# Values of a pair placed behind the next pair's scores, and the last values eight steps later

## The chip, the cores and the metric

The kernel runs on one core of a Trainium2 chip. The metric is the device time of one execution in microseconds (us). A core has a matrix engine (TensorE, PE in the profile, with its weight loads shown as PEld), a vector engine (VectorE, DVE), an activation engine (ScalarE, ACT), a general engine (GpSimd, POOL) and a sequencer that issues transfers (SyncE, SP). [...]

## The reference, cut to what matters

An attention over 4 batches, 8 heads, 768 tokens of 64 elements, followed by a Fourier mix and a two-layer network. Of the attention, per batch and head:

```python
block, window = (32, 16)
k_sum = k.reshape(B, H, nb, block, D).max(axis=3)
v_sum = v.reshape(B, H, nb, block, D).mean(axis=3)
scores_l = scale * q @ k.T        # kept where |i - j| < 16 ("near")
scores_s = scale * q @ k_sum.T + log(block)   # one column per block of 32 ("sums")
a = softmax(concat(scores_l, scores_s))
out = a @ concat(v, v_sum)
...
mixed = real(fft2(x)); u = x + mixed; un = layernorm(u)
result = u + relu(un @ w_ch1) @ w_ch2
```

All of it is in float32.

## The kernel before, in words

**What is threaded into what.** The heads of a batch are worked on in four pairs, g = 0 to 3. The attention of batch b + 1 is threaded into the dense layers of batch b. `gen_attention(b)` is a generator that is advanced step by step: every `yield` ends a step. For batches 2 and 3 the loop at the end, `drive((most, 44, 0), (gen_attention(b + 1), 80, 0))`, advances the dense work 44 steps while the attention takes 80. The dense steps are 16 of `gen_hidden(b, 0)` (tiles hx, hy, hz; line 1368), 12 of `gen_out(b, 0)` (tiles ox, oy, oz; line 1437; four steps for each of i = 0, 1, 2, with seven products in them) and 16 of `gen_hidden(b, 1)`. For batch 1 there is one attention step to five dense ones and ten of the conversion of the weights (`gen_weights`). After that stage `gen_out(b, 1)` and the Fourier mix of batch b + 1 (`gen_fourier`) run together.

**A pair.** `prepare` turns k and q (for batch 3 and all but the first pair of batch 2 with VectorE's transpose, line 711) and takes the block maxima. `scores(b, g)` makes the near scores: 48 matmuls on quarters of TensorE's array (64 rows by 64 columns, line 791) into two PSUM banks, an exp on ScalarE for each half (line 797) and a product with the mask `near` on VectorE. `sum_scores` makes the scores against the block maxima: four matmuls of 64 by 32 (tile ss, line 808) and an exp. `scale_sums` brings the block sums of v into place (tile vs: one matmul, line 814, and two scalings on ScalarE, line 816). `values(b, g, ...)` multiplies: 48 matmuls of 64 by 32 (tile av, line 826) with v from `vw_bufs`, six more with vs (line 831), then on VectorE two reciprocals and two products into x. `load_values` then issues four transfers on SP that refill `vw_bufs[g % 2]` for the pair after the next; they have to wait for that buffer's last reader.

**Buffers.** The attention's PSUM tiles (scores, ss, vs, av) share four banks (`abank`). The probabilities `p` have two buffers, `vw` two, `vs` one, and the natural q and k tiles four together.

**The order.** Apart from the first batch's attention, no order is written out by hand. A planner in the framework fixes each engine's order before the kernel runs: of the instructions that it believes ready, the one created first goes first. `tc.issue_after` adds an edge on one engine.

**The end of a batch's attention (b > 1).** After `values(b, 3)`, `turn_tiles` (lines 954 and 955) stores two tiles of x to DRAM on POOL's queue and gathers them back mirrored (tile xr). Some steps later `fold_batch` adds halves of x on VectorE, its second step reading xr; the Fourier mix needs the fold.

**Step numbers before, for batches 2 and 3**: scores at steps 5, 17, 27 and 37, values at 12, 22, 32 and 42, the fold from 59, its reader of xr at 60.

Of the kernel before, what the change touches and what calls it, by code (L numbers as in the profile page):

```python
# [488 lines left out]
def _main_program(ctx, tc, q, k, v, moe_w_ch1, moe_w_ch2, out):  # L489
# [9 lines left out]
    NP = H // 2  # L499
# [56 lines left out]
    def abank(shape, name):  # L556
        return psum.tile(shape, FP, tag="attn", bufs=4, name=name)
# [12 lines left out]
    def tt(out, in0, in1, op):  # L570
        return nc.vector.tensor_tensor(out=out, in0=in0, in1=in1, op=op).ins  # L571
# [92 lines left out]
    def load_values(b, g):  # L664
        if is_wide(b):
            load_wide_values(b, g)
            return
        load_narrow_values(b, g)

    def load_wide_values(b, g):  # L670

        vw, off = wide_vw(g), v[b, 2 * g].offset
        for r0, r1, i0, i1 in ((0, WK, 1, NQ - 1), (W, WK, 0, 1), (0, WK - W, NQ - 1, NQ)):
            for e in range(2):
                fetch(out=vw[r0:r1, e, i0:i1, 0:D],
                      in_=bass.AP(v.tensor, off + (S * e + QB * i0 - W + r0) * D,
                                  [[D, r1 - r0], [QB * D, i1 - i0], [1, D]]))

    def load_narrow_values(b, g):


        vw = vw_bufs[g % 2]
        if g < 2 and is_wide(b - 1):
            nc.gpsimd.memset(vw[:, :, D:D1], 1.0)
        for e in range(2):
            off = v[b, 2 * g + e].offset
            for h in range(2):
                r, i = 64 * (e ^ h), NB2 * h
                last = (b, g, e, h) == (B - 1, NP - 1, 1, 1)
                if last:  # L690

                    fetch(out=vw[r + 64 - W:r + 64, i:nb - 1, 0:D],
                                      in_=bass.AP(v.tensor, off + (BLOCK * i + 64 - 2 * W) * D,
                                                  [[D, W], [BLOCK * D, NB2 - 1], [1, D]]))
                n = 64 - W if last else 64
                fetch(out=vw[r:r + n, i:i + NB2, 0:D],
                                  in_=bass.AP(v.tensor, off + (BLOCK * i - W) * D, [[D, n], [BLOCK * D, NB2], [1, D]]))
# [104 lines left out]
    def sum_scores(b, g, p):  # L802
        km, qt = km_bufs[g % 2], nat[b, g]
        ps = abank([P, S2], f"ss_{b}_{g}")
        for h in range(2):
            for e in range(2):
                rows, r = slice(D * e, D * (e + 1)), 64 * (e ^ h) + 32 * h
                nc.tensor.matmul(ps[r:r + 32, :], km[rows, :], qt[rows, S2 * h:S2 * (h + 1)], start=True, stop=True)  # L808
        nc.scalar.activation(out=p, in_=ps, func=AF.Exp, scale=SC)

    def scale_sums(b, g):
        ps = abank([P, D], f"vs_{b}_{g}")
        vb, pick = sums[b, g]
        nc.tensor.matmul(ps, pick, vb, start=True, stop=True)
        for r in range(2):
            nc.scalar.activation(out=vs[:, r, 0:D], in_=ps, func=AF.Identity, scale=half_of[:, r:r + 1])

    def values(b, g, p, pm, x):
        vw = vw_bufs[g % 2]
        av = [abank([P, NST, D1], f"av_{b}_{g}_{r}") for r in range(2)]  # L820
        for t in range(NST):
            h = t // HT
            for j in range(4):
                for r in range(2):
                    rows, i = slice(64 * r, 64 * (r + 1)), 4 * t + j
                    nc.tensor.matmul(av[r][32 * j:32 * (j + 1), t, :], p[rows, h, i - NB2 * h, :], vw[rows, i, :],  # L826
                                     start=(t == 0), stop=False, skip_group_check=True)
        for t in range(HT):
            for r in range(2):
                rows = slice(64 * r, 64 * (r + 1))  # L830
                ins = nc.tensor.matmul(av[r][:, t:t + HT + 1:HT, :], pm[rows, P * t:P * (t + 1)], vs[rows],  # L831
                                       start=False, stop=(t == HT - 1), skip_group_check=True)
        marks["av", b, g] = ins.ins
        for r in range(2):
            rc = rec[:, b * NP + g, r]
            nc.vector.reciprocal(out=rc, in_=av[r][:, :, D])
            xo = x[:, 0, P * g + D * r:P * g + D * (r + 1)]
            xo = bass.AP(xo.tensor, xo.offset, [list(xo.ap[0]), [HT * DM + D * (1 - 2 * r), 2], [DM, HT], [1, D]])
            tt(xo, av[r].rearrange("p (h t) d -> p h t d", h=2)[:, :, :, 0:D],
               rc.rearrange("p (h t) -> p h t", h=2)[:, :, :, None].to_broadcast([P, 2, HT, D]), ALU.mult)  # L840
# [3 lines left out]
    def following(b, g, n):  # L844
        i = b * NP + g + n
        return divmod(i, NP) if i < B * NP else None
# [101 lines left out]
    def turn_tiles(b, x):  # L948


        xr = apool.tile([P, 2, NQ, QB], FP, tag="p", name=f"xr_{b}").rearrange("p e n c -> p (e n c)")
        back[b] = xr = xr[:, 0:2 * DM].rearrange("p (i d) -> p i d", i=2)
        turned = dpool.tile([P, 2, DM], FP, name=f"turned_{b}")
        nc.gpsimd.dma_start(out=turned, in_=x[:, 2:NST:HT, :])
        nc.gpsimd.indirect_dma_start(out=xr.rearrange("p i d -> p (i d)"), out_offset=None,
                                     in_=turned.rearrange("p i d -> p (i d)"),
                                     in_offset=bass.IndirectOffsetOnAxis(ap=mirror[:, 0:1], axis=0))
# [29 lines left out]
    def gen_attention(b):  # L987
        x = bpool.tile([P, NST, DM], FP, tag="x", bufs=2, name=f"x_{b}")
        x_of[b] = x
        held = None  # L990
        if b == 2:
            load(2, 1)
            load(2, 2)
        if b > 1:
            yield
            yield
            with tc.issue_after(marks["load"]):
                block_sums(b, 0)
            for _ in range(2):
                yield  # L1000
        for g in range(NP + 1):
            n1, n3 = (following(b, g, n) for n in (1, 3))
            if held:
                if b > 1:
                    scale_sums(b, g - 1)
                values(b, g - 1, *held, x)
                if n1 and b > 1:
                    load_values(*n1)
            if g == NP and b > 1:
                turn_tiles(b, x)  # L1010
                for _ in range(17):
                    yield
                rooms[b] = room(f"fold_{b}")
                steps = fold_batch(b, split_fold(b, rooms[b]))
                while True:
                    with tc.issue_after(marks["dense"]):
                        done = next(steps, steps) is steps
                    if done:
                        break
                    yield  # L1020
            elif held:
                for _ in range(5 if b > 1 else 1):
                    yield
            if g < NP:
                with tc.issue_after(marks["tile"]) if (b, g) == (1, 0) else ExitStack():
                    held = scores(b, g)
                if (b, g) == (1, 1):
                    with tc.issue_after(marks["mx", 0]):
                        key_maxima(g)
                sum_scores(b, g, held[1])  # L1030
            if g and n1 and b == 1:
                load_values(*n1)
            if g == 1 and b > 1:
                block_sums(b, 1)
            if g == NP and b > 1:
                return
            yield
            if g == NP:
                return
            for _ in range(2 if g == 0 and b > 1 else 0):  # L1040
                yield
            if (b, g) == (1, 0):
                for h in range(2):
                    with tc.issue_after(marks["un", 0]):
                        tt(held[0][:, h], held[0][:, h], near[:, h], ALU.mult)
            if n1:
                prepare(*n1, *((1,) if b > 1 else ()))
            if b == 1:
                scale_sums(b, g)
            if b > 1:  # L1050
                yield
                yield
                if n1:
                    prepare(*n1, 0)
            if n3 and not (b == 1 and n3 > (2, 0)):
                load(*n3)
            yield
            if b > 1:
                yield
# [561 lines left out]
```

## Time and profile before

| what | value |
|---|---|
| median of 3 runs | 794.84 us (793.83 to 795.17) |
| profiled execution, its own time | 793.7 us |
| span of the profiled execution | 791.9 us |
| busy: PE, DVE, ACT, POOL | 776.3, 492.0, 224.7, 47.9 us |
| PE busy in 274 to 375 us (attention of batch 2) | 100.72 of 101 us |
| PE busy in 460 to 525 us (attention of batch 3) | 64.48 of 65 us |
| near score matmuls, line 791 | 1152 records |
| value matmuls, lines 826 and 831 | 1152 and 144 records |

A float32 matmul leaves two records in the trace. Starts of matmuls are measured while their ends are modelled, so that in the timeline a group's duration runs over the next group's start; differences of starts are used below. In the page's chain of waits a share is the part of the span that belongs to an engine or a line on the chain of work that ended last. In a list of groups, "out<-in" names the tile that is written and those that are read.

### The profile page before, as it was taken

How to read it: one execution, taken by the hardware profiler on the slowest of the kernel's cores; microseconds unless marked ns; L12 is line 12 of the kernel's file. 1: busy time of each engine (PE TensorE's matmuls, PEld its weight loads, DVE VectorE, ACT ScalarE, POOL GpSimd, SP SyncE). 2: the span in 40 equal slices, each digit the busy share in tenths (PEclk: the TensorE clock that was granted, in tenths of full speed). 3: DMA queues.
4: the chain of work that ended last, by engine and by line, in shares of the span. 5: the costliest groups of instructions: out<-in, count | busy, mean ns of one | idle time of the engine just before them, and what ended most of it. 6: DMA issues, size and time to landing. Idle time of an engine off the chain costs nothing.

```text
span 791.9 us, 14352 instructions
## 1 busy us (share of the span) xinstructions
PE 776.3 (98%) x5920; PEld 562.9 (71%) x5920; DVE 492.0 (62%) x1019; ACT 224.7 (28%) x491; POOL 47.9 (6%) x85
## 2 busy tenths in 40 slices
PE   8998999999999999999999999999999999999997
PEld 6777655445588866787578866788569875886686
DVE  5899988787988556752758544653677623533352
ACT  3564757226525022100236012200226111001200
POOL 0000000000000020200210020300120000000000
PEclk9999999999999999999999999999999999999999
DMA  9999787695956179976342169610614153106001
GB/s 212 189 262 246 190 268 190 210 284 201 240 186 152 46 206 263 218 110 184 137 153 94 54 208 211 183 55 11 243 37 140 54 215 134 51 0 233 0 28 56
DMA packets 133353, 121.82 MB, mean 154 GB/s; under 512 B 94464, under 2 KB 114912, under 8 KB 133088
## 3 DMA queue, kind: packets, MB, share of 16 engines
q1 hardware_dynamic: 132160, 118.53, 54.0%
q0 software_dynamic: 576, 2.10, 0.8%
q8 instruction: 48, 0.79, 0.4%
q10 hardware_dynamic: 544, 0.20, 0.1%
q14 instruction: 25, 0.20, 0.1%
HBM read 97.22 MB, written 23.59 MB: 153 GB/s over the span
## 4 chain that ended last, share of the span: by engine, by line
PE 88%; DVE 5%; ACT 4%; DMA 2%; issue 1%; DVEq 0%
PE hx L1368 19%; PE ox L1437 18%; PE hz L1368 9%; PE oz L1437 9%; PE hy L1368 5%; PE o L1414 5%; PE oy L1437 5%; PE y L1252 3%; PE sc L791 2%; PE mx L1211 2%; PE av L826 2%; PE unt L1342 1%; PE av L831 1%; DMA qn<-in_q_dram 1%; PE ss L808 1%; ACT kt L727 1%
## 5 line engine op out<-in xcount | busy, mean ns | idle before, releaser
L1368 PE MATMUL hx<-u,w 128*128 128x384 f32 x512 | 185.4, 491 | 2.4 <-ACT h L1385 1.0
L1368 PEld LDWEIGHTS hx<-u,w 128*128 128x128 f32 x512 | 95.2, 190 | 71.3 <-ACT p L797 3.8
L1368 PE MATMUL hz<-u,w 128*128 128x384 f32 x256 | 93.0, 486 | 0.0
L1437 PE MATMUL oz<-w,s 128*128 128x256 f32 x336 | 81.3, 380 | 0.0
L1437 PE MATMUL ox<-w,s 128*128 128x256 f32 x336 | 80.1, 380 | 0.0
L1437 PE MATMUL ox<-w,h 128*128 128x256 f32 x336 | 79.6, 381 | 0.0
L571 DVE TENSOR_TENSOR x<-ox,x 128x256 f32<-128x256 f32 x84 | 35.5, 422 | 66.2 <-PE ox L1437 65.9
L1368 PEld LDWEIGHTS hz<-u,w 128*128 128x128 f32 x256 | 48.6, 190 | 33.9
L1437 PEld LDWEIGHTS ox<-w,h 128*128 128x128 f32 x336 | 63.1, 190 | 10.8 <-issue 1.2
L1437 PEld LDWEIGHTS ox<-w,s 128*128 128x128 f32 x336 | 63.2, 190 | 9.1 <-DVE x L571 0.3
L1437 PEld LDWEIGHTS oz<-w,s 128*128 128x128 f32 x336 | 63.3, 190 | 8.9 <-DVE x L571 0.4
L1379 ACT COPY h<-hx 128x384 f32<-128x384 f32 x32 | 15.3, 477 | 191.6 <-PE hx L1368 191.5
L571 DVE TENSOR_TENSOR h<-hy,h 128x384 f32<-128x384 f32 x32 | 17.8, 557 | 48.9 <-PE hy L1368 48.8
L1368 PE MATMUL hy<-u,w 128*128 128x384 f32 x128 | 46.8, 487 | 0.0
L571 DVE TENSOR_TENSOR h<-hx,h 128x384 f32<-128x384 f32 x32 | 17.8, 556 | 45.2 <-PE hx L1368 44.0
L1414 PE MATMUL o<-w,h 128*128 128x512 f32 x96 | 42.2, 595 | 0.7 <-DVE w L571 0.7
L1398 ACT ACTIVATE h<-hx 128x384 f32<-128x384 f32 x32 | 15.7, 489 | 89.4 <-PE hx L1368 89.4
L1437 PE MATMUL oy<-w,h 128*128 128x256 f32 x168 | 40.1, 380 | 0.0
L571 DVE TENSOR_TENSOR x<-oz,x 128x256 f32<-128x256 f32 x42 | 17.8, 423 | 30.4 <-PE oz L1437 30.1
L1368 PEld LDWEIGHTS hy<-u,w 128*128 128x128 f32 x128 | 24.2, 190 | 17.1 <-DVE h L571 0.7
L1437 PEld LDWEIGHTS oy<-w,h 128*128 128x128 f32 x168 | 31.8, 190 | 4.4
L1414 PEld LDWEIGHTS o<-w,h 128*128 128x128 f32 x96 | 18.0, 190 | 23.6 <-issue 20.7
(166 smaller groups left out, 1072.5 us busy)
## 6 DMA issues: line engine op xcount, KB each, us to landing
w<-dw SPq DMA_DIRECT2D x44, 896.0 KB, 5.6
words<-in_moe_w_ch_dram SPq DMA_DIRECT2D x32, 512.0 KB, 5.8
dw<-w SPq DMA_DIRECT2D x12, 896.0 KB, 7.0
vw<-in_v_dram SPq DMA_DIRECT2D x47, 192.0 KB, 6.2
out_dram<-x SPq DMA_DIRECT2D x23, 256.0 KB, 2.0
vb<-in_v_dram SPq DMA_DIRECT2D x24, 192.0 KB, 7.2
kn<-in_k_dram SPq DMA_DIRECT2D x9, 384.0 KB, 6.3
qn<-in_q_dram SPq DMA_DIRECT2D x9, 384.0 KB, 6.9
```

What stands on the lines that cost most here:

```text
L571: return nc.vector.tensor_tensor(out=out, in0=in0, in1=in1, op=op).ins
L727: nc.scalar.copy(out=dst[D * e:D * (e + 1), s:S:2], in_=ps[D * s:D * (s + 1)])
L791: nc.tensor.matmul(ps[h][r:r + 64, i, :], kt[rows, o:o + 64], qt[rows, o:o + BLOCK], start=True, stop=True)
L808: nc.tensor.matmul(ps[r:r + 32, :], km[rows, :], qt[rows, S2 * h:S2 * (h + 1)], start=True, stop=True)
L826: nc.tensor.matmul(av[r][32 * j:32 * (j + 1), t, :], p[rows, h, i - NB2 * h, :], vw[rows, i, :], start=(t == 0), stop=False, skip_group_ch ...
L1211: nc.tensor.matmul(out, y[:, g], table, start=False, stop=True, skip_group_check=True)
L1252: nc.tensor.matmul(y, fgs[b][par][:, st, P * g:P * (g + 1)], fs[par][:, g % 2, st, :], start=(st == 0), stop=(st == n - 1))
L1368: ins = nc.tensor.matmul(ps, w[:, a, kk, :], u[:, r, kk, :], start=start and kk == 0, stop=stop and kk == 1, skip_group_check=True)
L1379: nc.scalar.copy(out=c11, in_=X)
L1398: nc.scalar.activation(out=c21, in_=X, func=AF.Relu)
L1414: nc.tensor.matmul(ps, h[:, n, hf, P * t:P * (t + 1)], wt[2, b, j][:, 2 * hf:2 * hf + 2, :], start=(n, hf) == (0, 0), stop=(n, hf) == (NC ...
L1437: nc.tensor.matmul(ps, left[a][:, n, :], wt[2, b, j][:, r, :], start=start and n == 0, stop=stop and n == NC - 1, skip_group_check=True)
```

## The change

For the joined pairs (1 to 3 of batches 2 and 3, and pair 3 of batch 1) the values of the pair before are no longer issued ahead of the scores but behind `sum_scores`. For batches 2 and 3 `scale_sums` of that pair is then issued ahead of the scores, and `load_values` behind the values. The five steps between the old place and the scores stay, so that values 0, 1 and 2 go from steps 12, 22 and 32 to 17, 27 and 37. The last values of batches 2 and 3 wait eight steps more (42 to 50), `turn_tiles` with them, and the pause from there to the fold is nine steps instead of 17, so that the fold keeps its place.

```diff
         for g in range(NP + 1):
             n1, n3 = (following(b, g, n) for n in (1, 3))
-            if held:
+            joined = (1 if b > 1 else 3) <= g < NP
+            if b > 1 and g == NP:
+                for _ in range(8):
+                    yield
+            if held and not joined:
                 if b > 1:
                     scale_sums(b, g - 1)
                 values(b, g - 1, *held, x)
...
             if g == NP and b > 1:
                 turn_tiles(b, x)
-                for _ in range(17):
+                for _ in range(9):
                     yield
...
             if g < NP:
+                past = held
+                if joined and b > 1:
+                    scale_sums(b, g - 1)
                 with tc.issue_after(marks["tile"]) if (b, g) == (1, 0) else ExitStack():
                     held = scores(b, g)
                 if (b, g) == (1, 1):
                     with tc.issue_after(marks["mx", 0]):
                         key_maxima(g)
                 sum_scores(b, g, held[1])
+                if joined:
+                    values(b, g - 1, *past, x)
+                    if n1 and b > 1:
+                        load_values(*n1)
```

## The prediction

> **What bounds the kernel now.** I read the page first: the busy shares, then the chain that ended last.
>
> ```profile
> PE 776.3 (98%) x5920; PEld 562.9 (71%) x5920; DVE 492.0 (62%) x1019; ACT 224.7 (28%) x491; POOL 47.9 (6%) x85
> PE 88%; DVE 5%; ACT 4%; DMA 2%; issue 1%; DVEq 0%
> ```
>
> TensorE sets the time: 88% of the chain is its work. So the change is worth what it takes off TensorE's own row, or adds there. Next I read the timeline of TensorE where batch 2's attention is threaded through batch 1's dense work (274 to 375 us); columns are start, duration, engine, line, operation, count (two records a matmul).
>
> ```profile
> 281.32 1.45 PE L1368 MATMUL hz<-u,w 128*128 128x384 f32 x4
> 282.71 1.60 PE L791 MATMUL sc<-qt,kt 64*64 64x32 f32 x96
> 284.24 0.85 PE L808 MATMUL ss<-qt,km 64*32 64x384 f32 x8
> 285.02 1.56 PE L1368 MATMUL hx<-u,w 128*128 128x384 f32 x4
> 286.41 1.45 PE L1368 MATMUL hz<-u,w 128*128 128x384 f32 x4
> ...
> 292.86 1.45 PE L1368 MATMUL hz<-u,w 128*128 128x384 f32 x4
> 294.15 0.33 PE L814 MATMUL vs<-vbs,sel 96*128 96x64 f32 x2
> 294.42 1.20 PE L826 MATMUL av<-vw,p 64*32 64x65 f32 x96
> 295.55 0.94 PE L831 MATMUL av<-vs,p 64*128 64x130 f32 x12
> 296.42 1.56 PE L1368 MATMUL hx<-u,w 128*128 128x384 f32 x4
> ```
>
> Durations overlap, so I take differences of starts. A dense group of four records takes 1.29 us (292.86 to 294.15). Before a score visit it takes 1.39 (281.32 to 282.71): 0.10 to go in. After it, 1.39 again (285.02 to 286.41): 0.10 to come out. A score visit thus occupies 0.10 + 1.53 + 0.78 + 0.10 = 2.51 us. A value visit goes in at no visible cost and leaves at the same 0.10: 0.27 + 1.13 + 0.87 + 0.10 = 2.37.
>
> The same timeline at batch 2's last values shows a visit that has come apart:
>
> ```profile
> 353.88 0.33 PE L814 MATMUL vs<-vbs,sel 96*128 96x64 f32 x2
> 354.14 0.54 PE L826 MATMUL av<-vw,p 64*32 64x65 f32 x24
> 354.62 2.86 PE L1437 MATMUL ox<-w,h 128*128 128x256 f32 x12
> 357.41 0.88 PE L826 MATMUL av<-vw,p 64*32 64x65 f32 x48
> 358.22 0.93 PE L831 MATMUL av<-vs,p 64*128 64x130 f32 x6
> 359.08 1.13 PE L1437 MATMUL ox<-w,h 128*128 128x256 f32 x4
> 360.14 0.54 PE L826 MATMUL av<-vw,p 64*32 64x65 f32 x24
> 360.62 0.93 PE L831 MATMUL av<-vs,p 64*128 64x130 f32 x6
> ```
>
> From 353.88 to the next dense product at 361.48 are 7.60 us, in which lie 16 dense records of 0.216 (eight take 1.726 elsewhere), 3.45 us. The values cost 7.60 - 3.45 + 0.10 = 4.25 us where a whole visit costs 2.37. The planner cuts where it believes an operand isn't there; the cuts at 12 and 36 of 48 matmuls fit the four transfers of vw that these matmuls read.
>
> [...] That fits the broken visit: its first 12 matmuls take 0.48 us, 40 ns each, against 1.13/48 = 24 ns where both row halves alternate. [...] the two mask products take 2.76 us at 321.71, under four GpSimd additions (321.24 to 325.63), and 1.03 elsewhere.
>
> **The change part by part.** *Joining.* At pairs 1 to 3 of batches 2 and 3 the vs matmul (1), 48 + 6 value matmuls, and with them ACT's two scalings, DVE's two reciprocals and two products and SP's four vw loads go five steps later; only vs stands ahead of the scores. One way out (0.10) and one way in (0.10, vs taking dense-to-vs at nothing and vs-to-next at the 0.27 it has now) go: 6 x 0.20 = **-1.2 us**. Batch 1's values of pair 2 move from 144.87 to behind 166.55: **-0.15**, by the same rates.
>
> *Banks.* Four banks serve six tiles in a visit: vs, two scores, ss, two av. The first av takes the bank of vs, free after ACT's scalings (0.52 us) long before. The second takes the first scores' bank, free after an exp: that begins 0.11 after the scores (321.08 to 321.19) and takes 0.49, so it ends at 0.60, and ss covers 0.78. Margin 0.18. If it took the second exp (ends at 0.98 by 321.19 + 0.87 = 322.06), 0.20 a visit would show. Bounds 0 to 6 x 0.2 = 1.2; below nothing is excluded, as no such wait exists now. I take **+0.3**.
>
> *DVE and ACT behind the visit.* Reciprocals and products are 0.27 + 1.02 = 1.29 us. They begin when av ends, and the first dense group needs 1.39 us before DVE is wanted: hidden; were DVE late by the mask products, the next group's 1.29 still covers. One stall goes: at 324.99 TensorE waited for DVE, 1.73 instead of 1.29 after 323.26, **-0.44**; the av visit now stands there while DVE finishes. The like stall at 471.41 (batch 3, pair 0, not joined) stays.
>
> *SP.* vw(2,2) was issued from 304.37; it must now wait for av behind the scores that start at 303.06, to some 306.5: 2 us, with weight stores, weight loads and k and q loads behind it. Those k and q are for the next batch (460 us on), the weights for 326 on: cost 0, bound 1. vw(3,3), which held SP 8.6 us before the weight loads at 500.72, falls behind the weight load of dense step 13 (attention step 24, between old place 22 and new 27): a gain in slack only. In batch 1 the vw(2,0) loads (161.25 to 167.93) must wait for av to some 168.5; raw weights for DVE's conversion (168.03) stand behind. Bounds 0 to 2 us, the products "o" having waited for DVE w 2.5 us in all in that stage; I take **+0.3**.
>
> *Last values eight steps later.* Steps are 44 dense to 80: step 42 falls after 23 dense steps, step 50 after 27, both just ahead of an i's last product. The place is thus seven products later, ahead of the ox that starts at 370.38 now. vw(2,3) gets eight steps more, and asks at most five later, so I expect the visit whole: 4.25 - 2.37 = **-1.88**. What it risks is the turning on POOL:
>
> ```profile
> 362.69 0.87 POOL L954 DMA_DIRECT2D turned<-x  x1 [35.61 <-DVE x L571]
> 369.89 1.06 POOL L955 DMA_INDIRECT xr<-turned,mirror  x1 [6.33 <-DMA turned<-x]
> ```
>
> From the first to the gather's landing are 7.20 + 4.6 = 11.8 us; in batch 3 4.0 + 4.6 = 8.6. After the change the visit starts at 370.38 - 4.25 - 1.04 (0.6 of three joins, 0.44) = 365.1, ends 2.27 later, DVE 1.3 later, POOL starts near 369.0, xr lands near 380.8. DVE's reader of xr stands at 384.30 now and near 384.30 - 2.92 = 381.4 then: margin 0.6. If late, DVE's next products wait: 0.24 us is idle ahead of the one at 387.70, and TensorE covers 1.29 - 0.56 = 0.73 more. Bounds 0 to 1 (a landing 2 us later); I take 0, since nine steps remain. Nothing else on POOL is queued behind until the fold.
>
> **Sum**: -1.2 - 0.15 + 0.3 - 0.44 + 0.3 - 1.88 = -3.1 us. The profiled execution took 793.7 (span 791.9); it would take 790.6. The median shown is 794.84, 1.1 above it: **791.8 us**.
>
> **Rivals.** *The gains are eaten*: the last values stay apart (their loads move with them), or the margins of 0.18 and 0.6 fail. The joins alone are -1.2: 793.6, within 793.3 to 796.4. For it: the loads do move five steps. Against it: the last values move eight.
> *Visits come apart* (the slower side): with six tiles on four banks the planner finds av not ready after ss and puts dense products between, as at 354.62. The joined visit then does not exist. Each costs 1.88 more instead of 0.20 less. Two broken turn -3.1 into +1.1, not to be told from no change; three give 794.84 - 3.1 + 3 x 2.08 = 798.0, all six some 804. From three on the kernel is slower. For it: sc and ss had to part in batch 1 (82.52, 101.71), where banks were scarce. Against it: in batches 2 and 3 vs and av stay whole though av's last six wait for ACT, and only vw broke one.
>
> **Numbers.** Likeliest 0.58, its own range 790.0 (no bank or SP cost, and a little of the 471.41 stall) to 793.2. Eaten 0.21: 793.3 to 796.4. Apart 0.21: 796.4 to 804, half of it below 798. About 0.2% (1.6 us) is what a measurement of this kernel tells from no change. The range 790.0 to 798.0 leaves out the tail of the third case and a little below the first.
>
> **What would show it.** Right: in TensorE's timeline vs, sc, ss, av, av without a dense group between, six times; one way out each; the last av of batch 2 as x96; no gap at 324.99. Wrong: dense groups inside a visit, PE waiting for ACT p L797 ahead of av, or DVE fold waiting for xr.

## The result, and the profile after

The changed kernel takes **808.03 us** (median, 803.75 to 811.71) where the kernel before, run beside it, takes 795.0 (793.33 to 796.02): a ratio of 1.0158, 95% interval 1.0136 to 1.018. The prediction was 791.8, within 790.0 to 798.0. It was wrong: the kernel became slower by 13 us. The profiled execution took 807.59 us, with a span of 805.8 (before: 793.7 and 791.9). The six runs of the changed kernel spread over 1%, the six of the kernel before over 0.3%; 25 later ones of the kernel before spread over 0.9% (792.79 to 800.12).

The page after has these lines in the places of the two that the prediction began with (busy time of the engines; chain of work by engine), and between them, from the list of DMA queues, a line that was passed over before (packets, MB, share):

```profile
PE 778.3 (97%) x5920; PEld 566.7 (70%) x5920; DVE 491.9 (61%) x1019; ACT 225.0 (28%) x491; POOL 47.0 (6%) x85
...
q8 instruction: 48, 0.79, 0.4%
...
PE 86%; DVE 5%; ACT 4%; DMA 3%; issue 2%; SPq 0%; DVEq 0%
```

TensorE's work is the same, 778.3 us against 776.3, yet the span is 13.9 longer. So what was added is idle time, or time at a lower clock. "issue", waiting for nothing that the profile shows, has doubled to 2%. The list of TensorE's waits (waiting operation, what ended the wait, us in total, times, longest) says where:

```profile
PE hx L1379 <- DVE h L571: 4.5, 2, 3.9
PE av L826 <- issue: 3.9, 3, 2.5
PE av L831 <- issue: 3.5, 1, 3.5
```

Before, these were 0.8, 0.6 and none. First, though, the joins. A visit is a stay of TensorE at the attention's products between two groups of dense ones; in a joined visit it takes scores and values in one go. Here is TensorE's timeline in batch 2, the joined visit of pair 1, then that of pair 2, then the last values.

```profile
308.68 0.33 PE L814 MATMUL vs<-vbs,sel 96*128 96x64 f32 x2
308.94 1.60 PE L791 MATMUL sc<-qt,kt 64*64 64x32 f32 x96
310.48 0.85 PE L808 MATMUL ss<-qt,km 64*32 64x384 f32 x8
311.12 1.20 PE L826 MATMUL av<-vw,p 64*32 64x65 f32 x96
312.25 0.94 PE L831 MATMUL av<-vs,p 64*128 64x130 f32 x12
313.12 1.56 PE L1379 MATMUL hx<-u,w 128*128 128x384 f32 x4
...
326.63 0.85 PE L808 MATMUL ss<-qt,km 64*32 64x384 f32 x8
327.28 0.71 PE L826 MATMUL av<-vw,p 64*32 64x65 f32 x47
330.47 0.73 PE L826 MATMUL av<-vw,p 64*32 64x65 f32 x49 [2.48 <-issue]
...
375.44 1.20 PE L826 MATMUL av<-vw,p 64*32 64x65 f32 x96
```

The first visit is what the change was meant to bring: vs, sc, ss, av, av with no dense product between, 4.44 us to the next dense product and 0.11 for the way out, 4.55 in all, where two visits cost 2.51 + 2.37 = 4.88. The second stops for 2.5 us in the middle of 96 like records. The last line is batch 2's last value visit, now whole. Of the six joined visits of batches 2 and 3 five have this order. In the sixth, pair 3 of batch 3, the planner cut the scores in three, with dense products between:

```profile
520.36 0.31 PE L791 MATMUL sc<-qt,kt 64*64 64x32 f32 x6
...
523.39 0.41 PE L791 MATMUL sc<-qt,kt 64*64 64x32 f32 x10
...
530.84 1.37 PE L791 MATMUL sc<-qt,kt 64*64 64x32 f32 x80
```

By differences of starts these scores take 1.87 us instead of 1.53, with two more ways in and two more ways out (0.42): some 0.4 us more than a whole join saves. In batch 1 such a stop stands in the joined visit, and something follows it:

```profile
168.31 0.71 PE L831 MATMUL av<-vs,p 64*128 64x130 f32 x6
172.50 1.02 PE L831 MATMUL av<-vs,p 64*128 64x130 f32 x6 [3.48 <-issue]
173.45 13.44 PE L1425 MATMUL o<-w,h 128*128 128x512 f32 x28
186.73 1.45 PE L1379 MATMUL hx<-u,w 128*128 128x384 f32 x4
```

The 28 records of o are followed by the next group 13.28 us after their start. In the kernel before it was 12.12:

```profile
166.55 12.28 PE L1414 MATMUL o<-w,h 128*128 128x512 f32 x28
178.67 1.45 PE L1368 MATMUL hx<-u,w 128*128 128x384 f32 x4
```

A table by stretches (us of the stretch, busy time of TensorE, granted clock, DMA share, GB/s) shows why:

```profile
169.00:172.40 3.40, 0.02 (x1) 1.00 1.18 257
172.40:175.80 3.40, 3.30 (x9) 0.50 1.15 182
```

After a stretch of idleness TensorE ran one stretch at half its clock. The trace's clock records put the half-clock stretches of this execution, up to its last products, at 80.25, 172.41 and 582.01, each 3.41 us long, so each costs up to 1.71. The third follows the wait at batch 3's turned copy (timelines of GpSimd, VectorE and TensorE):

```profile
561.26 0.75 POOL L954 DMA_DIRECT2D turned<-x  x1 [51.23 <-DVE ok L1585]
571.48 1.03 POOL L955 DMA_INDIRECT xr<-turned,mirror  x1 [9.46 <-ACT h L1409]
...
578.56 0.69 DVE L571 TENSOR_TENSOR fold<-xr 128x512 f32<-128x512 f32 x1 [4.67 <-DMA xr<-turned,mirror]
...
582.24 4.41 PE L1379 MATMUL hx<-u,w 128*128 128x384 f32 x8 [3.86 <-DVE h L571]
```

From issuing the copy to having xr are 17.3 us (write 9.4 us to its landing, gather 7.1). In the kernel before it took 8.4 (the gather landed 4.4 us after its issue):

```profile
523.65 0.75 POOL L954 DMA_DIRECT2D turned<-x  x1 [21.98 <-DVE x L571]
527.65 1.03 POOL L955 DMA_INDIRECT xr<-turned,mirror  x1 [3.26 <-DMA turned<-x]
```

The **ledger** of the two profiled executions, 13.9 us apart in span:

| what | us |
|---|---|
| three gaps inside joined visits (3.48 + 2.48 + 0.79) | +6.75 |
| the wait for xr | +3.86 |
| two half-clock stretches, behind the gap of 3.48 and behind the wait for xr | +3.42 |
| before any moved product: waits for q until 40 us (1.2), the half-clock stretch at 80.25 (1.6) | +2.8 |
| five whole joins, 0.33 each | -1.65 |
| the sixth, cut | +0.4 |
| batch 2's last values | -1.88 |
| the stall at 324.99, gone | -0.44 |
| sum | 13.3 |

0.6 is not accounted for. The 2.8 belongs to the execution rather than to the change: up to 144.87 of before TensorE's products stand in the same order in both kernels, and a version without any join (below) has a half-clock stretch at 78.22 too.

### The profile page after: what moved, and what is told of

The parts are those of the page before. It is cut to its first block, busy times and chain, and to the rows that moved or that the text cites. A ratio compares the mean times of both kernels' runs of the same rounds, so it can differ in the third digit from the quotient of the medians.

```text
span 805.8 us, 14349 instructions
## 1 busy us (share of the span) xinstructions
PE 778.3 (97%) x5920; PEld 566.7 (70%) x5920; DVE 491.9 (61%) x1019; ACT 225.0 (28%) x491; POOL 47.0 (6%) x85
## 4 chain that ended last, share of the span: by engine, by line
PE 86%; DVE 5%; ACT 4%; DMA 3%; issue 2%; SPq 0%; DVEq 0%
PE hx L1379 19%; PE ox L1448 18%; PE hz L1379 9%; PE oz L1448 9%; PE hy L1379 5%; PE o L1425 5%; PE oy L1448 4%; PE y L1263 3%; PE sc L791 2%; PE mx L1222 2%; PE unt L1353 2%; PE av L826 1%; PE av L831 1%; DMA words<-in_v_dram 1%; PE ss L808 1%
## 5 line engine op out<-in xcount | busy, mean ns | idle before, releaser
L1379 PEld LDWEIGHTS hy<-u,w 128*128 128x128 f32 x128 | 24.2, 190 | 17.1 <-DVE h L571 0.7
```

The source lines that it names most:

```text
L1379: ins = nc.tensor.matmul(ps, w[:, a, kk, :], u[:, r, kk, :], start=start and kk == 0, stop=stop and kk == 1, skip_group_check=True)
```

## The experiments

**Theory A** (instruction blocks). The profile page's 48 instruction packets of 16,384 B serve TensorE, which has 11,967 records, 11,840 of them weight loads and products: at 256 instructions a packet, 46.7. A joined visit holds 107 matmuls, two product and two load records each, 428 instructions in 4.5 us. In the trace all three gaps lie at one place of the count, at instruction number 193 or 194 over a multiple of 256 (a block is what one packet brings, and ends there), and end 1.3 to 1.7 us after an instruction packet has landed. So TensorE had used up a block before the next had come. In all twelve profiles the n-th packet lands before block n + 2 starts, in those of the kernel before and of the changed one by 1.2 us or more. **Theory B** (late turn). Batch 3's turned copy, pushed from 523.65 to 561.26, meets five weight loads of 896 KB that SP issues from 560.35. **Rivals**: C, the last values are late in themselves; D, av waits for something of the program (a bank, vw, an exp).

### Joins taken out, last values late

```
-            joined = (1 if b > 1 else 3) <= g < NP
+            joined = False
```

> The joins are taken out (values of a pair ahead of the next pair's scores again); the last values stay eight steps later. Theory A, instruction blocks: the loss sits in joined visits, where 428 TensorE instructions run in 4.5 us and a block of 256 is used up in some 2.4 us, before the next has come; without joins no visit holds a whole block, so no gap over 0.5 us stands ahead of av, and batch 2's last values gain 1.88. Theory B, late turn of batch 3: without joins the planner puts batch 3's attention earlier, so its gather starts while SP is quiet and the 3.86 us wait on DVE goes as well. Both give 791 to 794. Rival C, the last values being late is itself the loss (x of batch 2 or 3 late): 798 or more, DVE waiting for xr.

Measured: 793.45 us against 795.63, ratio 0.9966 (0.9952 to 0.998). Of the gaps of av by "issue" only the 0.6 us of before is left, and xr is waited for nowhere. C falls for batch 2. This is the part of the change that works: it is **2.2 us faster than the kernel before** (0.2 to 0.48%), about the 1.88 of batch 2's last values. The split isn't measured: the stalls at 324.99 and 471.41 (0.44 and 0.52 us) are absent from its profile too. Batch 3's last values come early here, as its attention runs ahead of the dense work once nothing is joined, so this run doesn't separate A from B.

### Joins kept, last values in their old place

```
             if b > 1 and g == NP:
-                for _ in range(8):
+                for _ in range(0):
...
-                for _ in range(9):
+                for _ in range(17):
```

> The joins stay in all seven places; the last values stand in their old place (batch 2's come apart again, as before: +1.88 against the changed kernel). Theory A: gaps without a shown cause inside joined visits remain, each 0.7 to 3.5 us, at instruction numbers that lie near 193 over a multiple of 256; 3 to 8 us in all. Theory B: the turn of batch 3 is issued some 8 steps earlier (12 us), so of 3.86 + 1.67 at most 2 us are left. A and B together: 799 to 805. Only B true (no loss in joins): 794 to 796. Only A true: 807 to 811.

Measured: 804.11, ratio 1.0116 (1.0081 to 1.0151). Four gaps inside joined visits, 7.1 us together by the list of waits (av "issue" 4.2 and 3.5, of which 0.6 is there in all versions), two half-clock stretches behind them (168.84 and 329.26), and no wait for xr: the copy is issued at 549.97, its gather lands in 4.3 to 4.6 us. Against the kernel before, the joins alone cost some 9 us (8.5 by the medians, 9.2 by the ratio).

### Values behind the next scores, but apart from them

```
-                for _ in range(5 if b > 1 else 1):
+                for _ in range((3 if joined else 5) if b > 1 else (0 if joined else 1)):
...
                 if joined:
+                    for _ in range(2 if b > 1 else 1):
+                        yield
                     values(b, g - 1, *past, x)
```

> As the changed kernel (the values of a pair come after the next pair's scores, last values eight steps later), but with four dense products (two in the visit of batch 1: none to twenty) between the sum scores and the values: nothing is joined, each part stays below 256 instructions. Theory A: no gap over 0.5 us ahead of av; the 3.48 + 1.16 + 2.48 + 0.79 us of the changed kernel go, six entries and exits of 0.33 come back. Theory B: the wait for batch 3's turn stays, 3.9 + 1.7. Together 799 to 803. Rival D, the values' late place itself (a bank that an exp frees, vw that comes late) makes the gaps: they stay, 806 to 811.

Measured: 802.07, ratio 1.0076 (1.0048 to 1.0104). The time is as theory A had it, the picture is not. The gaps of batches 1 and 3 are gone, that of batch 2's pair 2 is shorter (1.74 us instead of 2.48), and pair 1's visit, which ran through in the changed kernel, has one of 0.86 (TensorE's timeline):

```profile
307.72 0.79 PE L826 MATMUL av<-vw,p 64*32 64x65 f32 x53 [0.86 <-issue]
...
326.25 0.73 PE L826 MATMUL av<-vw,p 64*32 64x65 f32 x49 [1.74 <-issue]
```

They stand again at numbers 194 and 193 over a multiple of 256. A part of the visit below 256 instructions, as the expectation put it, is the wrong measure: the block reaches from the scores over four dense products into the values and lasts 5.2 us (301.48 to 306.65), and the packet landed 4.9 us after its beginning. What counts is the time for 256 instructions, wherever the visits are cut. The wait for xr is there as theory B has it: 2.5 us on TensorE, with a half-clock stretch at 579.99.

### The block boundaries moved

```
-        keep_busy(3, p[NP - 1][:, 0].rearrange("p n c -> p (n c)"))
+        keep_busy(35, p[NP - 1][:, 0].rearrange("p n c -> p (n c)"), 44)
```

> As the changed kernel, with 32 small products (64x64 by 64x44, 128 TensorE instructions, about 1.5 us, result not used) added at some 42 us, long before any joined visit: the order of all else is the same, and every block boundary lies 128 instructions earlier in the program. Theory A: gaps in joined visits stand again at instruction numbers of about 193 over a multiple of 256, so at other operations than now (128 instructions away from the old ones) or in other visits, and some of the three old ones are gone; time 803 to 813. Rival D (bank, vw, exp): the gaps stand at the same operations of the same visits, with the same lengths.

Measured: 815.08, ratio 1.0237 (1.02 to 1.0274). The 35 products, in the trace 128x128 by 128x44 and not 64x64 as expected, took 13.77 us, not the 1.5 expected for 32 more, with half the clock from 44.31 to 61.38, so the total is above the range. What the run was for came out: 49 packets instead of 48, and the gaps are elsewhere, at numbers 193 and 194 again. There are five; three of them:

```profile
320.65 0.38 PE L831 MATMUL av<-vs,p 64*128 64x130 f32 x1 [0.80 <-issue]
...
338.79 0.48 PE L1379 MATMUL hx<-u,w 128*128 128x384 f32 x1 [0.45 <-issue]
...
359.40 0.34 PE L826 MATMUL av<-vw,p 64*32 64x65 f32 x12 [1.96 <-issue]
```

Batch 1's joined visit now runs through. Batch 2's joined visits of pairs 1 and 3 stall, and that of pair 3 ran through in the changed kernel and in the one with joins only. Behind pair 2's visit it is a dense product (hx) that stalls, with no av in it. In order, program and data these visits are those of the changed kernel. D falls: nothing that av waits for in the program was touched.

### Scores issued twice, nothing joined

```
-        for i in range(NB2):
+        for i in list(range(NB2)) * (2 if b > 1 else 1):
             for h in range(2):
                 o = BLOCK * (NB2 * h + i)
...
-            joined = (1 if b > 1 else 3) <= g < NP
+            joined = False
```

Batch 3's last values are in their old place.

> The version without joins (batch 2's last values late, batch 3's in their old place), in which every score product of batches 2 and 3 is issued twice into the same place: no value product is moved, no wait added, only 48 products of 64x64 by 64x32 (192 TensorE instructions) more in each of eight visits, 400 in sc and ss together. Cost by the rate of the profile, 8 x 1.53 = 12.2 us on 793.5: 805.7. Theory A: a whole block again lies in a stretch of some 4 us, so gaps without a shown cause appear inside sc or ss, at numbers of 193 or 194 over a multiple of 256, 1 to 3 us each in two to five visits, perhaps with half-clock stretches: 808 to 818. If the gaps come from the values' place or from the joins as such: no gaps, 804.5 to 806.5.

Measured: 830.13, ratio 1.0464 (1.0421 to 1.0507), 24 us above the 805.7 that the products themselves account for, and above the range of theory A, which had the sign and the place right and the size too low. TensorE's timeline at the first doubled visit:

```profile
282.80 2.75 PE L791 MATMUL sc<-qt,kt 64*64 64x32 f32 x172
290.95 0.85 PE L791 MATMUL sc<-qt,kt 64*64 64x32 f32 x20 [5.40 <-issue]
```

There are four such gaps (3.2 to 5.6 us between starts), in sc or at ss, all at numbers 193 and 194, and 23.9 us of half-clock stretches beside them. No value product was moved and no wait added. The added instructions, 8 x 192 = 1536, brought six more packets (54): 256 each. This settles theory A: the **number of instructions in a short time** makes the gap, not the join as such. In the twelve profiles together 35 gaps of 0.15 us or more stand at block boundaries, and every one of them ends 1.15 to 1.66 us after its packet has landed.

The trace's instruction packets beside these gaps (times in us; "left" is when TensorE leaves a block and begins the one just ahead of the packet's own, "runs" is the first product of the next, "gap" is from start to start):

```
kernel          left    packet           runs     after landing  gap
changed, b1     166.01  169.97 - 170.84  172.50   1.66           3.75
changed, b2     309.21  308.31 - 309.38  311.54   2.17           none
changed, b2     325.44  327.83 - 328.95  330.47   1.52           2.70
changed, b3     508.60  509.62 - 510.64  511.97   1.33           1.00
apart, b2       301.48  305.08 - 306.42  307.72   1.30           1.07
boundary moved  355.04  356.50 - 358.04  359.40   1.36           2.18
scores twice    283.44  288.37 - 289.43  290.95   1.52           5.62
scores twice    484.86  488.92 - 490.00  491.37   1.38           4.65
```

In the rows with a gap a packet sets out 1 to 5 us after TensorE has left a block, takes 0.9 to 1.5, and its block runs 1.3 to 1.7 later. A joined visit uses a block up in 2.3 to 2.4 us (309.21 to 311.54). The second row escaped because the packet had set out 0.9 us before: there the boundary lies some 40 instructions behind the visit's start, and the dense products ahead of it gave the time. Such early packets are common (200 of 559 in the twelve profiles, all but four while dense or other long products run), but none set out more than 44 instructions ahead. In the kernel before, the shortest block of batches 1 to 3 lasts 3.83 us (512.86 to 516.69) and its packet came in time, 1.81 us before need.

### Batch 3's last values back in their old place

```
             if b > 1 and g == NP:
-                for _ in range(8):
+                for _ in range(8 if b == 2 else 0):
...
-                for _ in range(9):
+                for _ in range(9 if b == 2 else 17):
```

> As the changed kernel, but batch 3's last values (and with them its turned copy) stand in their old place, eight steps earlier; batch 2's stay late, all joins stay. Theory B: the turned copy and its gather no longer meet the five weight loads of 896 KB each; landing in 4 to 5 us each instead of 9.4 and 7.1, no wait for xr, so 3.86 us of waiting and the half-clock stretch behind it (1.71) go: 808.0 - 5.6 = 802.4, within 801 to 804. If the wait for xr has another cause than the late place, it stays and the time is 806 or more.

Measured: 803.52, ratio 1.0109 (1.0067 to 1.0151). The copy is issued at 551.90, write and gather land in 3.2 and 4.2 us, no wait for xr and no half-clock stretch near 582 remain, as theory B had it. In this profile the gaps are longer, 9.4 us between starts in four.

### Four of the five weight loads left out

```
     def get_w2(b, j):
+        if b == 2 and j >= NC:
+            wt[2, b, j] = wt[2, b, j - NC]
+            return
```

> As the changed kernel, but four of the five weight loads that SP issues at 560.35 are left out: in batch 2's dense work the second products of blocks 4 to 7 read the weights of blocks 0 to 3 (that part is computed with other weights). TensorE's order, the joins and the late place of the last values are the same. Theory B, the turned copy is slowed by those loads: it lands in 4 to 5 us instead of 9.4, the gather in 4 to 5 instead of 7.1, the wait for xr (3.86) and the half-clock stretch behind it (1.71) go: 802.5, within 801 to 804. If the late place alone makes it late, the landings become shorter by less than 3 us in all and a wait of over 2 us stays: 805 or more.

Measured: 804.24, ratio 1.0088 (1.0057 to 1.0118). GpSimd's timeline:

```profile
562.93 0.75 POOL L954 DMA_DIRECT2D turned<-x  x1 [48.91 <-DVE ok L1588]
566.94 1.03 POOL L955 DMA_INDIRECT xr<-turned,mirror  x1 [3.26 <-DMA turned<-x]
```

The copy is as late as in the changed kernel, but lands in 3.2 us instead of 9.4, the gather in 4.3 instead of 7.1, and nobody waits for xr. Theory B holds: it is the meeting with the weight loads that makes the turn 17 us long, and the eight steps that bring it there. C falls for batch 3 too: the place is as late, and nothing waits. The time lies just above the expected 801 to 804; in this profile two gaps (3.75 and 3.05 us) were each followed by 6.83 us at half clock.

### No join in batch 1; and both repairs at once

```
-            joined = (1 if b > 1 else 3) <= g < NP
+            joined = b > 1 and 1 <= g < NP
```

> As the changed kernel, but batch 1's single join is taken out. Theory A: the 3.48 us gap ahead of av at 172.50 and the half-clock stretch behind it (1.71) go, an entry and an exit (0.33) come back: 808.0 - 4.9 = 803.1, within 801.5 to 804.5; gaps of batches 2 and 3 and the wait for xr stay. If the start of batch 1's dense work would have stalled anyway (o waiting for weights), less than 2 us are won.

Measured: 801.84, ratio 1.0108 (1.0062 to 1.0154). Batch 1's gap and the stretch behind it are gone; the wait for xr stays (2.7 us on TensorE); gaps of 1.10 and 3.52 us remain in batch 2 and one of 1.15 in batch 3, with a half-clock stretch at 327.98 behind the longest.

With this and with batch 3's last values in their old place:

> Both at once: batch 3's last values in their old place and no join in batch 1; six joins in batches 2 and 3 and batch 2's late last values stay. If the terms add: 808.0 - 5.6 - 4.9 = 797.5, within 796 to 800, what is left being the gaps in the joined visits of batches 2 and 3 (2.48 + 0.79[...]) less the six joins' 2.0 and batch 2's 1.9. Were the joins of batches 2 and 3 worth their 2.0 us without loss, it would be 791.5.

Measured: 796.27, ratio 1.0018 (1.0001 to 1.0036). The terms add. The six joins of batches 2 and 3 still have three gaps (0.82, 1.41 and 0.80 us between starts), none followed by a half-clock stretch, and the kernel is where it was before the change, within 0.4%. Beside 793.45 with no join at all, the six joins still cost some 2.8 us.

### Joins only where the block boundaries allow them

```
-            joined = (1 if b > 1 else 3) <= g < NP
+            joined = (b, g) in ((2, 3), (3, 1))
```

Batch 2's last values are late, batch 3's in their old place.

> The version without joins (batch 2's last values late, batch 3's in their old place), with two joins put back: values of pair 2 behind the scores of pair 3 in batch 2, and values of pair 0 behind the scores of pair 1 in batch 3. In the changed kernel these two visits stand so to the block boundaries (a boundary within some 40 instructions of the visit's start, the next block already there or nearly so) that none of the runs showed a gap in them. Theory A: no gap here either, and each join saves its entry and exit: 793.45 - 2 x 0.33 = 792.8, within 791.5 to 794. If a join stalls wherever it stands: 1 to 3 us each, 795 to 799.

Measured: 793.39, ratio 0.9966 (0.9951 to 0.9981). Both joined visits run through (vs at 482.23 to the next dense product at 486.67: 4.44 us, as at 308.68 above) and the list of TensorE's waits has no gap in them. As theory A has it, a join stalls by its place in the count of instructions; with the boundaries moved, the first of these two visits had stalled as well (359.40 above). That two joins save 0.66 can't be seen in the medians: 793.39 here, 793.45 with no join.

## Why the prediction was wrong, step by step

*Last values, batch 2: -1.88.* Held. The visit is whole (375.44, x96), 2.37 us with its way out; the version without joins gains 2.2, in which some of the stalls' share may lie.

*Joining: -1.2.* Right for a visit that runs through, and there too small: it saves 0.33, since besides a way out and a way in ss and av overlap, 0.64 us from start to start (310.48 to 311.12) instead of 0.78. Five visits were whole, the sixth was cut. *Stall at 324.99: -0.44.* It is gone (hx follows hz after 1.29 us, 333.40 to 334.69), but in the version without joins too (325.54 to 326.83), so the reason given, that av stands there meanwhile, is not shown.

*Banks: +0.3, SP: +0.3.* Neither was needed. av follows ss at 0.64 to 0.65 in the joined visits shown, so no exp was waited for; o's wait for DVE's w is 0.8 us instead of 0.7.

**The step that failed first** is the sum for a joined visit itself: it adds the durations of two visits and takes away a way in and a way out, as if TensorE could always go on at that rate. It has no term for the supply of instructions. That term measured 6.75 us in gaps and up to 1.71 in one half-clock stretch in the changed kernel's profile, and the joins with nothing else cost 9 us net where the prediction had -1.2. *Batch 1: -0.15* has the same flaw at its worst: 3.48 us of gap and the half-clock stretch.

**The second step that failed** is the turn of batch 3. The prediction worked out batch 2's margin of 0.6 (which held: no wait for xr there, which landed at 390.9 and was read at 391.6) and gave batch 3 only the chain of before, 8.6 us (8.4 by its trace), without placing it beside SP's queue at its new time. It measured 17.3, and 3.86 us of waiting and up to 1.71 of half clock showed on TensorE. It asked what is queued behind the copy on GpSimd, not what the other queues send while the copy is under way.

A third term was missing behind both: **a gap costs more than itself**. In these profiles every gap that left TensorE idle for 2.3 us or more of one 3.41 us stretch was followed by one or two stretches at half clock, up to 1.71 us each. Below 2 us it went both ways: 1.72 and 1.74 us were followed by one, 1.70 and 1.83 were not, and at 78 to 80 us six executions had one behind 1.3 to 1.6 us in several pieces.

*Rivals.* "Visits come apart" gave the slower side and the times 796.4 to 804, by a mechanism that did not make the loss: the planner cut only the scores of batch 3's last joined visit, for some 0.4 us, and 808.03 lies above its range. "Gains are eaten" failed too. Of the signs of being wrong one came true, DVE's fold waiting for xr. No case named the supply. The profile of before held the hint, in batch 0 and in the list of waits: 0.5 us of sc (L748) by "issue", a gap that ends at 27.58 among small products, 1.35 us after an instruction packet's landing. It was not followed up.

*Left open.* What makes a packet set out at once or 5 us late. Of the packets in all twelve profiles that set out behind TensorE's step to a new block, the median delay is 1.0 us where the other queues kept the DMA engines under 5% busy in the 3 us before (48 packets) and 2.9 where over 95% (215), so traffic may have a part, but no run changed the traffic alone at a gap. The gap at one and the same place, in the visit of batch 2's pair 2, also differs between the versions that join it (1.19 to 3.31 us idle); whether that makes the changed kernel's runs spread is not shown. Nor is it known why the added products of the boundary experiment kept the clock at half for 17 us, or what decides where a stretch is idle for less than 2 us.

## What to carry to other kernels

Count instructions, not only their time: find the stretches where 256 TensorE instructions (64 fp32 matmuls, with two products and two weight loads each) run in less than some 5 us (behind the joined visits and doubled scores the blocks with a gap lasted 2.1 to 5.4 us without it), and keep longer products between such stretches rather than packing them together. Idle time "by issue" amid like products is the sign; the instruction packets in the trace date it. When a step is moved, put its transfers beside everything that the other queues issue at the new time, and price an idle gap of about 2 us or more with the half-clock stretch that may follow (up to 1.71 us each here).

## What the runs showed that was not expected

- Half-clock stretches begin at whole multiples of 3.41 us from one another (80.25, 172.41 and 582.01 are 27 and 120 stretches apart), so a gap's **place** has a part in what follows. In the kernel with batch 3's values early, a gap of 2.77 us (330.34 to 333.11) fell across a boundary at 331.84, 1.5 us to one side and 1.3 to the other, and no half-clock stretch followed. In the one with joins only, of a gap of 2.23 us 1.72 lay within one stretch (325.85 to 329.26) and the next ran at half clock (0.50). A stretch of 3.41 us that was idle for about half was enough in two cases (1.72 and 1.74 us).
- In these profiles no packet set out more than 44 instructions before TensorE began the block just ahead of the packet's own: hardly more than one block was all the cover that a fetch had, 2.3 us in a joined visit (309.21 to 311.54) and over 20 in dense work (24.2 to 36.6 from 589.39 to 773.99 in the changed kernel).
- A 512 KB copy from GpSimd's queue landed in 3.2 us on quiet queues and in 9.4 beside five weight loads of 896 KB; the gather behind it in 4.2 to 4.4 and in 7.1.
